# Reordered steps at the hand-over from the first token group to the second: weight sums, streamed forms, token statistics

## The chip, the cores and the metric

The kernel runs on one core of a Trainium2 chip. The metric is the device time of one execution in microseconds (us). TensorE is called PE in the profile, VectorE DVE, ScalarE ACT, GpSimd POOL and SyncE SP. SP issues nearly all of the DMAs in this kernel. Each engine works through one queue in order, so an instruction that waits holds up all that stand behind it on its engine.

## The reference

Windowed attention with four sink tokens feeds a Fourier mix, a layer norm and a feed-forward net:

```python
# q, k, v: (4, 8, 768, 64) fp32; window 128, 4 sinks
a = softmax(mask(q @ k.T / 8));  x = (a @ v)            # as (4, 768, 512)
u = x + real(fft(fft(x, axis=1), axis=2))
un = (u - mean(u)) / sqrt(var(u) + 1e-6)                # per token
out = u + relu(un @ w_ch1) @ w_ch2                      # w_ch1 (512, 2048), w_ch2 (2048, 512)
```

There are 3072 tokens, which the feed-forward net takes as 6 groups of 4 blocks of 128 tokens. The products are worked out in fp32 precision: each operand is split into a high half and a low half (what the high half lacks), and each product takes three matmuls (high by high, high by low, low by high).

## The kernel before

**The stages.** Attention and the Fourier mix come first, and their tail overlaps the first blocks of the feed-forward net. The first token group (group 0) runs a loop `for f in range(NF)` over 16 blocks of 128 hidden units. A step of the loop multiplies block f (`ch1`, L703: 12 matmuls of 128x512, tile `h`, reading the group's transposed tokens `un_slots` and the weights' two halves `w_ring`), splits the result (`split`: L1192 on ACT writes the relu's high half into `h_sb`, L1193 on DVE the low half) and multiplies block f-1 by the second weight matrix (`ch2`, L1199: 12 matmuls, tile `o`).

**Weights in the same loop.** The raw weights come from HBM by SP (L621, three buffers `raw`) two steps ahead. `convert` works on each: three DVE instructions (L639, L640, L641), the high half on ACT (L650 for the first matrix into `w_ring`, L665 for the second into `w`), the low half on POOL (L651, L666). A later group doesn't use the first matrix itself but seven sums of its quarters ("forms", a Strassen-like scheme with 7 products in place of 8). So `combine_w1(p)` takes the pair p of blocks f = 2p and 2p+1: four POOL instructions on 256 columns (L677 to L680) write the sums `tq` from `tw`, and a step later `halves` splits them into `to` (ACT L685, POOL L686). L687 stores these to HBM (`wd`), L654 stores `w_ring` there.

**The second group's tokens.** `prepare_1` is a generator of 20 steps that readies group 1 while group 0 runs: four of statistics (DVE L530, L531), one of the deviation (`deviations`, L537 to L552, with one square root on ACT, L540, and the load of its table ahead of it), then for each block a normalisation on ACT (`un_make`, L562, L563) and a transposition (PE L571, tile `unt`; ACT copies it out at L1257 into `xf`), and seven of sums of the token quarters (`do_x`: DVE L1301 the sums, ACT L1295 the high halves, DVE L1298 the low halves `x`). From f = PREP on, each step of the loop takes three of them.

**Group 1.** From `with tc.manual_schedule()` on, the order of the program is that of the engines; before it, a scheduler sets the order on each engine, held only by edges such as `tc.issue_after`. Four passes (`it`) of seven products each (`product`, L1421: 12 matmuls of 128x256 into the banks pA, pB and pC) read one form each, which two DMAs of 256 KB stream from HBM into one of eight places (L1394; `w_c` in the former raw buffers, `w_t`, `w_q` and `w_h` in the former `to`, `tq` and `h_sb`). The DVE combines the products (L1535 to L1559), `halves` splits them into `hring`, which takes the memory of `un_slots`, and `unit` (L1449, 12 matmuls, tile `o`) multiplies by the second matrix. After the products come numbered steps, ten in a pass: `todo` has the statistics, the deviation, the normalisation (`make`, L565 on DVE) and the transposition (`turn`) of group 2; `w2_at` has sums of the second matrix (DVE L1469, POOL L1474 to L1477, ACT L1481, POOL L1482) for the groups after that. Groups 2 to 5 work with streamed forms too (L1421, L1598).

## Time and profile before

| what | us |
|---|---|
| median of 3 runs (lowest, highest) | 746.86 (746.4, 748.05) |
| the profiled execution, its own time | 747.63 |
| its span in the trace | 745.9 |
| PE busy | 715.6 (96%) |
| DVE busy | 560.5 (75%) |
| ACT busy | 357.3 (48%) |
| POOL busy | 274.4 (37%) |

1.73 us of the profiled execution lie outside the span. Times in the trace count from the span's start. "PEld" is the loading of weights into PE, which runs beside the matmuls; "SPq" is SP issuing a DMA. The granted PE clock, as a mean over the span, was 0.994 of full speed. A bracket at the end of a row of the timeline says how long the engine had been idle before the row and what it then waited for. PE is the engine with the most work by far, so the question for any change is where PE is idle, and for what.

### The profile page before, as it was taken

The numbers are of one execution on the slowest core, as the hardware profiler recorded it, in microseconds if no ns is written. First come the engines' busy times: TensorE is split into PE (matmuls) and PEld (weight loads), VectorE is DVE, ScalarE is ACT, GpSimd is POOL, SyncE is SP. The second block draws the span as 40 slices with busy tenths as digits, with TensorE's granted clock in tenths as the row PEclk, the third lists the DMA queues.
The fourth block names the chain that finished last, engine by engine and source line by source line (L and its number), as shares of the span: only waits on it lengthen the run. The fifth ranks groups of instructions, "written<-read, shape, count | busy, mean of one in ns | idle before, by whom it ended". The sixth has DMA issues, their size and how long they took to land.

```text
span 745.9 us, 15695 instructions
## 1 busy us (share of the span) xinstructions
PE 715.6 (96%) x5539; PEld 642.6 (86%) x5539; DVE 560.5 (75%) x1299; ACT 357.3 (48%) x901; POOL 274.4 (37%) x391
## 2 busy tenths in 40 slices
PE   8999998989979999898999999999999999999996
PEld 6776876867868888687989999999999999999996
DVE  7778578888899988858668667947697578846773
ACT  5887666766634537313324134534444245523541
POOL 3567467577557989824994000000000000000000
PEclk9999999999999999999999999999999999999998
DMA  9863525533207999779999798979974897759721
GB/s 304 289 173 106 149 73 165 174 94 103 86 21 237 328 346 330 277 277 385 374 301 327 246 348 277 313 239 379 375 242 167 321 378 261 255 205 390 269 98 62
DMA packets 109576, 181.69 MB, mean 244 GB/s; under 512 B 9868, under 2 KB 44812, under 8 KB 108336
## 3 DMA queue, kind: packets, MB, share of 16 engines
q1 hardware_dynamic: 109200, 176.83, 69.6%
q0 software_dynamic: 288, 3.76, 1.3%
q8 instruction: 46, 0.75, 0.4%
q14 instruction: 42, 0.34, 0.1%
HBM read 148.04 MB, written 32.51 MB: 242 GB/s over the span
## 4 chain that ended last, share of the span: by engine, by line
PE 50%; DVE 4%; ACT 1%; issue 1%; SPq 0%; DMA 0%; POOL 0%; DVEq 0%
PE pB L1421 10%; PE qB L1598 9%; PE pA L1421 7%; PE pC L1421 6%; PE qC L1598 6%; PE qA L1598 6%; PE o L1449 5%; DVE bn L530 1%; PE unt L571 1%; DVE hring L1193 0%; DVE x L1657 0%; DVE x L1660 0%; SPq L1394 0%; DVE un L565 0%; DVE stat L531 0%
## 5 line engine op out<-in xcount | busy, mean ns | idle before, releaser
L1620 ACT CAST hring<-x 128x512 fp32r<-128x512 f32 x92 | 57.0, 619 | 52.0 <-PE qB L1598 19.6
L811 ACT ACTIVATE sm<-sm,mx 128x132 f32<-128x132 f32 x192 | 75.9, 400 | 4.6 <-DVE mx L805 4.6
L1624 DVE TENSOR_TENSOR hring<-x,hring 128x512 fp32r<-128x512 f32 x92 | 63.4, 689 | 14.8 <-ACT hring L1620 9.3
L786 PE MATMUL s<-ring,q 64*128 64x260 f32 x320 | 49.0, 411 | 5.9 <-DVE mx L805 2.7
L805 DVE CUSTOM_DVE_ANT_0 sm<-s,mask 128x132 f32<-128x132 f32 x192 | 48.5, 293 | 6.2 <-DVE s L792 0.9
L703 PE MATMUL h<-un_slots,w_ring 128*128 128x512 f32 x192 | 49.7, 405 | 3.4 <-POOL w_ring L651 2.9
L703 PEld LDWEIGHTS h<-un_slots,w_ring 128*128 128x128 f32 x192 | 36.3, 194 | 12.4 <-POOL w_ring L651 4.1
L786 PEld LDWEIGHTS s<-ring,q 64*128 64x128 f32 x320 | 26.9, 185 | 18.2 <-issue 5.0
L1598 PE MATMUL qA<-w,hring 128*128 128x256 f32 x312 | 39.8, 279 | 0.0
L1449 PE MATMUL o<-w,hring 128*128 128x512 f32 x156 | 38.5, 393 | 1.3 <-ACT hring L1192 1.1
L850 ACT COPY pta<-pt 128x512 f32<-128x512 f32 x48 | 28.1, 585 | 24.1 <-PE pt L843 24.0
L881 PE MATMUL xt<-ptl,ldv 128*64 128x128 f32 x384 | 39.3, 285 | 0.0
L1199 PE MATMUL o<-w,h_sb 128*128 128x512 f32 x156 | 38.1, 392 | 0.0
L1598 PEld LDWEIGHTS qA<-w,hring 128*128 128x128 f32 x312 | 37.9, 189 | 0.0
L811 ACT ACTIVATION_READ_ACCUMULATOR sm<-sm,mx 128x1 f32 x192 | 36.7, 191 | 0.0
L792 DVE COPY_PREDICATED s<-older,s 128x256 f32<-128x256 uint8 x80 | 33.7, 421 | 3.1 <-PE s L786 3.1
L859 POOL TENSOR_SCALAR_AFFINE_SELECT ptl<-pta 128x512 f32<-128x512 f32 x48 | 31.5, 655 | 11.6 <-ACT pta L850 11.6
L1598 PE MATMUL qB<-w_c,hring 128*128 128x256 f32 x288 | 35.2, 281 | 0.0
L1449 PEld LDWEIGHTS o<-w,hring 128*128 128x128 f32 x156 | 28.5, 188 | 7.5 <-ACT hring L1192 1.3
L881 PEld LDWEIGHTS xt<-ptl,ldv 128*64 128x64 f32 x384 | 22.1, 136 | 14.6 <-issue 4.8
L1598 PEld LDWEIGHTS qB<-w_c,hring 128*128 128x128 f32 x288 | 34.5, 189 | 0.0
L1199 PEld LDWEIGHTS o<-w,h_sb 128*128 128x128 f32 x156 | 29.1, 188 | 6.1
(296 smaller groups left out, 1965.3 us busy)
## 6 DMA issues: line engine op xcount, KB each, us to landing
w_c<-wd SPq DMA_DIRECT2D x96, 256.0 KB, 5.0
w_h<-wd SPq DMA_DIRECT2D x76, 256.0 KB, 5.1
w_t<-wd SPq DMA_DIRECT2D x70, 256.0 KB, 4.7
raw<-in_moe_w_ch_dram SPq DMA_DIRECT2D x32, 512.0 KB, 4.5
w_c<-td SPq DMA_DIRECT2D x48, 256.0 KB, 4.6
w_q<-wd SPq DMA_DIRECT2D x38, 256.0 KB, 5.0
wd<-to SPq DMA_DIRECT2D x8, 1024.0 KB, 6.4
ldv<-in_v_dram SPq DMA_DIRECT2D x28, 256.0 KB, 3.3
```

The costliest lines, as they stand in the source:

```text
L703: T.matmul(ps[:, :tb], a[cc], x[:, :, cc, :], start=n == 0, stop=n == 3 * NCC - 1)
L786: T.matmul(ps[:, j, :P + W], st["q", g][rows, hp, :], keys(g, 2 * hp + j), start=True, stop=True)
L792: V.copy_predicated(ps[:, :, P + NS:P + W], older[qi > 2], ps[:, :, 0:P])
L805: V.tensor_tensor_reduce(sm[:, h % 4], ps[:, j, P:P + W], mask[min(qi, 3)], -SCALE, 3.0e38, ALU.add, ALU.min, accum_out=mx[:, 0, h:h + 1])
L811: A.activation(sm[:, h % 4], sm[:, h % 4], AF.Exp, bias=mx[:, 0, h:h + 1], scale=-1.0, accum_out=mx[:, 1, h:h + 1])
L881: T.matmul(ps[D * j:D * j + D, p, :], st["v", kb(g) - i][:, h, :], a[:, h % 4, :], start=i == 0, stop=i == n - 1)
L1199: T.matmul(po[i], a[:, P * i:P * i + P], x, start=f == 0 and n == 0, stop=f == NF - 1 and n == 2)
L1421: T.matmul(ps[:, 256 * j:256 * j + 256], w[:, j, a, cs], x[:, xs], start=BANK.index(BANK[k]) == k and j == c == m == 0, stop=j == c == 1 a ...
L1449: T.matmul(po[i], h[:, a, j, ts_], x, start=first and j == m == 0, stop=last and j == 1 and m == 2)
L1598: T.matmul(ps[:, 256 * t:256 * t + 256], h[:, a, j, P * t:P * t + P], x, start=BANK.index(BANK[k]) == k and c == t == j == m == 0, stop=c ...
L1620: A.copy(hi, x)
L1624: V.tensor_tensor(*args, op=ALU.subtract)
```

## The change

It has four parts.

1. The steps of `prepare_1` are spread by a table: none in the step of f = 12, and the seven sums of the token quarters at f = 13 to 15 rather than up to f = 12. Each step is issued no earlier than the latest relu on ACT and the latest low half on DVE.
2. `combine_w1` issues its sums behind the low half of block 2p+1 on POOL, and two sums of 256 columns become one of 512. There are three instructions (L679, L680, L681 in the new kernel) for four.
3. The first four streamed forms (NH = 4) are loaded into `hring`, the memory of `un_slots`, as soon as `ch1` of the last block has read it, and not into `w_c` and `w_t`. The next three go to `w_c`. The last stores (`w_ring` and `to` of the last pair) stand on SP behind these seven forms. The order of the places after that is `w_q`, `w_t`, `w_t`, `w_h`.
4. Group 2's statistics, square root, normalisation and transposition move from the steps 0 to 14 to the steps 3 to 24, so that its first transposition stands in the second pass.

How this moves POOL at the blocks f = 12 and 13 (`tw_4007` before, `tw_3992` after; `tq` and `to` are the sums and the halves of the pair): before,

```order
L651 TENSOR_TENSOR w_ring<-tw_4007,w_ring 128x2x256
L677 TENSOR_TENSOR tq_4090<-tw_4007 128x256
L679 TENSOR_TENSOR tq_4090<-tw_4007 128x256
L678 TENSOR_TENSOR tq_4090<-tw_4007,tq_4090 128x256
L651 TENSOR_TENSOR w_ring<-tw_4007,w_ring 128x2x256
L680 TENSOR_TENSOR tq_4090<-tw_4007,tq_4090 128x256
L666 TENSOR_TENSOR w_1_4075<-cv_4067,w_0_4074 128x512
L666 TENSOR_TENSOR w_1_4087<-cv_4078,w_0_4086 128x512
L686 TENSOR_TENSOR to_4091<-tq_4090,to_4091 128x2x256 x2
L651 TENSOR_TENSOR w_ring<-tw_4131,w_ring 128x2x256
```

and after, with the two halves of the pair before (`to_3951`) parted:

```order
L687 TENSOR_TENSOR to_3951<-tq_3950,to_3951 128x2x256
L651 TENSOR_TENSOR w_ring<-tw_3992,w_ring 128x2x256
L687 TENSOR_TENSOR to_3951<-tq_3950,to_3951 128x2x256
L651 TENSOR_TENSOR w_ring<-tw_3992,w_ring 128x2x256
L679 TENSOR_TENSOR tq_4074<-tw_3992 128x512
L680 TENSOR_TENSOR tq_4074<-tw_3992,tq_4074 128x256
L681 TENSOR_TENSOR tq_4074<-tw_3992,tq_4074 128x256
L666 TENSOR_TENSOR w_1_4059<-cv_4051,w_0_4058 128x512
L666 TENSOR_TENSOR w_1_4071<-cv_4062,w_0_4070 128x512
L687 TENSOR_TENSOR to_4075<-tq_4074,to_4075 128x2x256
L651 TENSOR_TENSOR w_ring<-tw_4113,w_ring 128x2x256
L687 TENSOR_TENSOR to_4075<-tq_4074,to_4075 128x2x256
```

Both low halves of the first matrix now stand ahead of the pair's sums; before, three of the four sums stood between them. The low half of the next block (`tw_4113`) stands behind one half of the sums' split now, and behind both before.

On SP at the end of the first group (`wd_69` and on are the stored weights in HBM), before:

```order
L687 DMA wd_75<-to_4091 128x2048
L654 DMA wd_76<-w_ring 128x1536
L1394 DMA w_c_4268<-wd_69 128x512
L1394 DMA w_c_4268<-wd_70 128x512
L687 DMA wd_76<-to_4200 128x2048
L1394 DMA w_c_4269<-wd_69 128x512
L1394 DMA w_c_4269<-wd_70 128x512
```

and after, from the last of the eight loads into `hring` on (they stand right behind the store of `to_4075`):

```order
L1356 DMA hring<-wd_70 128x512
L1356 DMA w_c_4266<-wd_69 128x512
L1356 DMA w_c_4266<-wd_70 128x512
L1356 DMA w_c_4267<-wd_69 128x512
L1356 DMA w_c_4267<-wd_70 128x512
L1356 DMA w_c_4268<-wd_69 128x512
L1356 DMA w_c_4268<-wd_70 128x512
L654 DMA wd_76<-w_ring 128x1536
L688 DMA wd_76<-to_4179 128x2048
L1356 DMA w_q<-wd_71 128x512
```

The second form's loads no longer stand behind the store of the last pair's sums.

On PE at block 9 of the first group, where group 1's first transposition (`unt_0`) stands, before:

```order
L1199 MATMUL o_0_3243<-w_1_3706,h_sb_3788 128x512
L1199 MATMUL o_0_3244<-w_1_3706,h_sb_3788 128x512
L571 MATMUL unt_0_3895<-ident,un_4_3842 128x128 x4
L703 MATMUL h_9_3910<-un_slots,w_ring 128x512 x12
L1199 MATMUL o_0_3241<-w_0_3810,h_sb_3858 128x512
```

and after:

```order
L1200 MATMUL o_0_3243<-w_1_3703,h_sb_3784 128x512
L1200 MATMUL o_0_3244<-w_1_3703,h_sb_3784 128x512
L704 MATMUL h_9_3899<-un_slots,w_ring 128x512 x3
L571 MATMUL unt_0_3890<-ident,un_4_3837 128x128 x4
L704 MATMUL h_9_3899<-un_slots,w_ring 128x512 x9
L1200 MATMUL o_0_3241<-w_0_3806,h_sb_3853 128x512
```

It has moved three matmuls back on PE. What it reads has moved further on the other engines: group 1's square root (ACT L540, with its table load) stood behind the relu of block 3 in the before kernel, and stands between the relus of blocks 7 and 8 now. Group 2's square root stood on ACT ahead of the relu that feeds the first `unit`; now it stands behind the four relus of the first pass. Group 2's `unt_0` stood on PE behind the first `unit`; now it stands behind the third.

The diff, cut to its core:

```diff
-PREP_N = 3
+PREP_N = {6: 3, 7: 3, 8: 2, 9: 2, 10: 2, 11: 1, 13: 2, 14: 2, 15: 3}
...
-                    G.tensor_tensor(d[1], tf, f32(d[0]), op=ALU.subtract)
+                    state["lo", f] = G.tensor_tensor(d[1], tf, f32(d[0]), op=ALU.subtract).ins
...
-                G.tensor_tensor(q[:, 1], b12, b11, op=ALU.subtract)
+                with tc.issue_after(state["lo", 2 * p + 1]) if p else ExitStack():
+                    G.tensor_tensor(q[:, 1:3], t[:, 1].rearrange("p (h c) -> p h c", h=2), t[:, :, :256], op=ALU.subtract)
                 G.tensor_tensor(q[:, 0], b22, q[:, 1], op=ALU.subtract)
-                G.tensor_tensor(q[:, 2], b22, b12, op=ALU.subtract)
                 G.tensor_tensor(q[:, 3], b21, q[:, 0], op=ALU.subtract)
...
+            NH = 4
+            def place(n):
+                return hring[:, n] if n < NH else places[(n - NH) % NWS]
...
                 ps = hp.pop(0) if f < 2 else ch1(0, f, unT0)
+                if f == NF - 1:
+                    hring = npool.tile([P, 4, 2, 2, 256], F32R, tag="un_slots", name="hring", bufs=1)
+                    for n in range(NH):
+                        load(n)
...
-                for _ in range(PREP_N if f >= PREP else 0):
-                    next(steps, None)
+                for _ in range(PREP_N.get(f, 0)):
+                    with tc.issue_after(state["h_lo"]), tc.issue_after(state["relu"]):
+                        next(steps, None)
...
+            with tc.issue_after(state["load"]):
+                for n in range(NH, NH + LDB):
+                    load(n)
             for i in sorted(stores):
-                for fn in stores.pop(i):
-                    fn()
+                with tc.issue_after(state["load"]) if i > 2 * NF else ExitStack():
+                    for fn in stores.pop(i):
+                        fn()
...
-                    load(n + NWS)
+                    if n >= NH:
+                        load(n + NWS)
...
-                todo = {0: [(statistics, 0)], 1: [(statistics, 1, 2)], 2: [(statistics, 3)], 3: [(deviate, 7)], 5: [(deviate,), (make, 0)],
-                        7: [(turn, 0, *banks[1][:2]), (make, 1)], 9: [(turn, 1, *banks[1][:2]), (make, 2)],
-                        12: [(turn, 2, *banks[0][:2]), (make, 3)], 14: [(turn, 3, *banks[0][:2])]}
+                todo = {3: [(statistics, 0)], 4: [(statistics, 1)], 6: [(statistics, 2)], 7: [(statistics, 3)], 8: [(deviate, 1)],
+                        9: [(deviate, 1)], 10: [(deviate,)], 11: [(make, 0)],
+                        12: [(turn, 0, *banks[0][:2]), (make, 1)], 14: [(turn, 1, *banks[0][:2]), (make, 2)],
+                        22: [(turn, 2, *banks[1][:2]), (make, 3)], 24: [(turn, 3, *banks[1][:2])]}
```

## The prediction

> **What bounds the kernel now.** I read the page's chain by engine first, then the windows of busy time, then what PE waited for between 215 and 350 us, and last the timelines of PE, POOL, DVE, ACT and SP there.

> ```profile
> PE 50%; DVE 4%; ACT 1%; issue 1%; SPq 0%; DMA 0%; POOL 0%; DVEq 0%
> ...
> 350.00:400.00 50.00, 50.00 (x320) 45.02 (x319) 37.00 (x37) 16.91 (x29) 48.71 (x44) 1.00 1.02 339
> ...
> PE h L703 <- POOL w_ring L651: 2.9, 2, 1.5
> PE pB L1421 <- DMA w_c<-wd: 1.3, 1, 1.3
> PE o L1449 <- ACT hring L1192: 1.1, 1, 1.1
> ...
> PE pB L1421 <- ACT xf L1257: 1.0, 1, 1.0
> ```

> The chain is PE. The second line is a window (length, then busy us of PE, weight loads, DVE, ACT and POOL, then clock, DMA share, GB/s): behind 350 PE has nothing to gain. The wait lines (total, times, longest) name four causes at the hand-over, which are the places that the change touches. There PE's idle time counts in full, since behind it PE runs without gaps. PE itself shows what each costs, as extra time from one start to the next:

> ```profile
> 277.06 2.92 PE L1199 MATMUL o<-w,h_sb 128*128 128x512 f32 x12
> 279.82 0.60 PE L571 MATMUL unt<-ident,un 128*128 128x128 f32 x4
> ...
> 292.56 2.99 PE L703 MATMUL h<-un_slots,w_ring 128*128 128x512 f32 x12
> ...
> 305.95 2.56 PE L703 MATMUL h<-un_slots,w_ring 128*128 128x512 f32 x10 [1.36 <-POOL w_ring L651]
> ...
> 313.23 2.56 PE L703 MATMUL h<-un_slots,w_ring 128*128 128x512 f32 x10 [1.49 <-POOL w_ring L651]
> ...
> 318.39 2.93 PE L703 MATMUL h<-un_slots,w_ring 128*128 128x512 f32 x12
> ...
> 326.67 1.58 PE L1421 MATMUL pA<-x,w_c 128*128 128x256 f32 x12
> 329.55 1.69 PE L1421 MATMUL pB<-x,w_c 128*128 128x256 f32 x12 [1.30 <-DMA w_c<-wd]
> ...
> 332.50 1.59 PE L1421 MATMUL pA<-x,w_t 128*128 128x256 f32 x12
> 333.93 1.57 PE L1421 MATMUL pB<-x,w_t 128*128 128x256 f32 x12
> ...
> 339.90 0.60 PE L571 MATMUL unt<-ident,un 128*128 128x128 f32 x4
> ...
> 346.27 1.61 PE L1421 MATMUL pA<-x,w_h 128*128 128x256 f32 x12
> 348.85 1.68 PE L1421 MATMUL pB<-x,w_c 128*128 128x256 f32 x12 [0.96 <-ACT xf L1257]
> ```

> Twelve matmuls of 128x512 take 2.76 us from start to start (277.06 to 279.82), twelve of 128x256 1.43 (332.50 to 333.93).

> **The change, part by part.** *Sums behind the low halves.* From 292.56 to 318.39 PE does eight sets of 2.76, 22.08 us, in 25.83: 3.75 lost, in the main before `h`'s third matmul, twice. The cause stands on POOL and DVE:

> ```profile
> 301.20 1.06 POOL L677 TENSOR_TENSOR tq<-tw 128x256 f32<-128x256 f32 x1 [2.48 <-DVE tw L641]
> ...
> 304.62 1.28 POOL L651 TENSOR_TENSOR w_ring<-tw,w_ring 128x512 fp32r<-128x512 f32 x1
> ...
> 309.37 2.57 POOL L686 TENSOR_TENSOR to<-tq,to 128x512 fp32r<-128x512 f32 x2
> ...
> 313.12 0.75 POOL L677 TENSOR_TENSOR tq<-tw 128x256 f32<-128x256 f32 x1
> ...
> 294.04 1.82 DVE L1301 TENSOR_TENSOR xf<-xf 128x512 f32<-128x512 f32 x1
> ...
> 300.39 0.67 DVE L641 SCALAR_TENSOR_TENSOR tw<-raw,cw 128x512 int32<-128x512 int32 x1
> ```

> Block 13's converted weight is there at 301.06 (300.39 + 0.67). Three sums, 301.20 to 304.62, then stand ahead of its low half, which ends at 305.90; PE goes on at 305.95. Even with the DVE as late as this, the low half behind an ACT cast (0.6) would now end at 301.06 + 0.6 + 1.28 = 302.9, while PE wants it at 305.95 - 1.36 = 304.6. That wait goes. For block 14, POOL then has the wide sum (1.28, as for 512 columns in L651), two sums at 0.75, two low halves of the second matrix at 1.3, one half of `to` at 1.28 and the low half itself, 1.28: 7.9 us, so 310.8, against PE's need, the 1.36 earlier, at 313.23 - 1.49 - 1.36 = 310.4. With the DVE as late as before, 0.4 of the 3.75 would stay. But the x sums that stand ahead of this conversion leave it: three of L1301's form lie between 294.04 and 300.39, at up to the first one's 1.82, so the conversion is some 3 to 5 us earlier, and the wait is gone. I take 3.75; bounds 3.3 to 3.75. The merged sum saves some 0.2 us of POOL, which is off PE's path.

> *The first forms into `hring`.* 326.67 to 329.55 is 2.88, so 1.45 over a product. The chain of waits shows what released it:

> ```profile
> 322.60 1.27 POOL to L686
> ...
> 324.72 0.93 SPq L1394
> ...
> DMA to landing us min/median/max: 5.2/5.2/5.2
> ...
> DMA to landing us min/median/max: 3.4/3.4/3.4
> ```

> The second form's load stood on SP behind the store of POOL's last split, which ended at 323.87. From issue to landing it took 5.2 us (the first landing line; the second is the first form's, 7 us earlier). Now SP waits only for the last `ch1`, which ends two sets, 5.52 us, before the first product. With 3.4 to landing the first form is there 2 us early or so. The seven forms then have to keep up: at the 339 GB/s of the window, 512 KB take 1.55 against a product of 1.43, so 0.8 us is lost over seven forms, within the lead. At the spacing of the row of 324.72 (0.93 a DMA) the tenth would be issued 8.4 us after the first and land at 11.8, while the fifth form is wanted at 5.52 + 5.72 = 11.2: 0.6 us late. I take 1.45, bounds 0 to 1.45. The late stores of `wd_76` are read in pass 3 only, 40 us later; that lag is their cover.

> *Group 2's steps later.* 333.93 + 1.43 = 335.36, and the unit's 2.76 would end at 338.12, but `unt` starts at 339.90: 1.78 lost. Group 2's square root on ACT waited for its statistics, with the relu behind it; now it stands behind the relus. And from 346.27 to 348.85 1.15 over a product was lost, since the second pass's pB took the bank of `unt_1` while ACT's copy was outstanding; that transposition now lies in pass 2 and in the other bank. Bounds 1.4 to 1.78 and 0.6 to 1.15 (the DVE still has the statistics there); I take the full values.

> Gains: 3.75 + 1.45 + 1.78 + 1.15 = 8.1 us.

> *Cost one: group 1's `unt_0` within block 9.* Before, PE got to it at 279.82 and its normalisation was long done. Now:

> ```profile
> 243.88 1.28 ACT L540 ACT_TABLE_LOAD   x1
> 245.17 0.21 ACT L540 ACTIVATE stat<-stat 128x4 f32<-128x4 f32 x1
> ...
> 254.98 0.73 ACT L563 ACTIVATE un<-un,stat 128x512 f32<-128x512 f32 x1 [0.46 <-DVE stat L552]
> ...
> 276.53 0.69 DVE L639 TENSOR_SCALAR cw<-raw 128x512 int32<-128x512 int32 x1 [0.72 <-DMA raw<-in_moe_w_ch_dram]
> ...
> 269.11 0.43 SPq L621 DMA_DIRECT2D raw<-in_moe_w_ch_dram  x1
> DMA to landing us min/median/max: 4.2/5.5/7.2
> ```

> The deviation now follows block 8's first conversion on the DVE, which I put at 276.4: the DVE did this conversion just before the row at 276.53, and one more statistic of group 1 stands beside it. Table load 1.28, root 0.21: 277.9. Then block 8's relu on ACT (0.6) and four tiny DVE steps among block 8's conversions, which take 2 us each: the factor is there at 281.0, and one pass of `un` (0.73) ends at 281.8. PE is at `unt_0` three matmuls after 279.82, at 280.5. Wait 1.3; bounds 0 (the DVE idled 0.72 here, so it may come earlier) and 3.0 (where that load lands after 7.2 us and not the 5.5 of the median).

> [...]

> *Cost two: group 2's `unt_0` behind the third unit.* PE is there 9 products and 3 units after the first product's start T0: 12.87 + 8.28 = 21.15. Its normalisation waits on this:

> ```profile
> 347.69 0.63 ACT L1192 ACTIVATE hring<-tmp 128x512 fp32r<-128x512 f32 x1 [3.12 <-DVE tmp L1559]
> ...
> 348.69 1.14 ACT L1481 CAST tmp<-tmp 128x512 fp32r<-128x512 f32 x2
> 349.74 0.59 ACT L1533 COPY tmp<-pA 128x512 f32<-128x512 f32 x1
> ...
> 350.63 0.69 DVE L1535 TENSOR_TENSOR tmp<-pB,tmp 128x512 f32<-128x512 f32 x1 [1.13 <-PE pB L1421]
> ```

> The pass's last relu started 21.0 after T0 = 326.67, of which PE's stalls are 3.2: T0 + 17.8. The root (0.21) and two casts (1.14) and the copy (0.59) follow the relu's 0.63 on ACT, then the DVE's 0.69 and a normalisation, 0.54 where nothing disturbs it: T0 + 21.6. Statistics that now lie later in the pass may add 1, normalisations that leave it take off up to 1.5. I take a wait of 0.8, bounds 0 and 3.

> Net: 8.1 - 1.3 - 0.8 = 6.0. The profiled execution's 747.63 becomes 741.6 (span 745.9 to 739.9, 1.73 around it unchanged); it stands 0.77 above the median, so the median should come to 746.86 - 6.0 = 740.9.

> **The rivals.** (a) Both transpositions are ready in time: gain 8.1, 738.8. For it: the DVE's free time; against it: each chain above ends behind PE by its rows.
> (b) The streamed forms still come late by the 1.45 lost now: 742.3. For it: the DMA engines are busy all through (a share of 1.02 in that window) and the spacing of 0.93; against it: the lead of 5.5 us.
> (c) The x sums, now at f = 13 to 15, meet POOL's last sums, and the low halves of x are late for the first product: 1.82 for 0.68 three times is 3.4 us more DVE there; about half uncovered gives 1.7, so 742.6. For it, L1301 at 1.82 beside a POOL at work, and L677 at 1.06 then and 0.75 alone.
> [...]
> (d) POOL's sums of the second matrix set the pace of group 1. POOL is busy 48.71 of the window's 50 us and PE doesn't wait, but PE comes some 4 us earlier against them. If ACT's casts behind POOL then hold its relus, up to 2.5 of that is given back: 743.4.
> (e) ACT stands still behind the table load for as long again (1.28): 742.2. Against it: the root's start at 245.17, right behind the load's end. [...]
> (f) The parts cancel within what a measurement of this kernel can tell, 0.2% (1.5 us): the two new waits at their upper bounds, 3.0 and 3, and (b) as well would leave 0.7.
> (g) Slower, by one mechanism: `unt_0` in block 9. Its chain hangs on a raw load issued at 269.11, with 4.2 to 7.2 us to landing (5.5 as a median), then DVE, table load, DVE, ACT. PE can't pass it, so each us costs one. The gain is gone when `un` comes 6.0 us after 281.8, at 287.8, and it is slower by over 0.2% from 289.3. The spread of landings gives 1.7 only (7.2 for 5.5); it would need the DVE and ACT steps to lie behind a further block's conversions.

> **How the numbers follow.** My forecast 0.41 (own range 739.5 to 742.4), (a) 0.16, (b) 0.11, (c) 0.06, (d) 0.09, (e) 0.02, (f) 0.07, (g) 0.08. Faster by over 0.2%: the first six, 0.85; within: (f), 0.07; slower: (g), 0.08. The range goes from 738.2, (a) with a little more from an emptier DVE in the attention's tail (two L530 leave it), to 745.0, 1.6 above (d) for the costs' upper bounds; (f) and (g) lie outside.

> **What the profile would show.** Right: no PE wait on L651's successor after 300 us; the loads into `hring` issued right after the last `ch1`, no wait on a DMA in the first seven products; the first unit without a wait on a relu; waits before `unt` of 1.3 near 281 and 0.8 at T0 + 21. Wrong: a gap of over 3 us at one of these transpositions, waits of the products on forms or on x, or waits of group 1's units on ACT behind POOL's sums.

## The result, and the profile after

The changed kernel is slower. Its median is 758.34 us (755.94 to 759.84, 6 runs) against 747.1 (746.4 to 751.21, 6 runs) for the kernel before on the same chip: a ratio of 1.0145, interval 1.0123 to 1.0167, some 11 us where 6 us less were forecast. The profiled execution took 759.84 with a span of 758.1, so the two traces differ by 12.2 us of span. All times below "in the trace" are of such single profiled executions.

The page of the changed kernel, its busy times first and then its chain by engine:

```profile
PE 720.9 (95%) x5539; PEld 647.7 (85%) x5539; DVE 563.8 (74%) x1299; ACT 356.6 (47%) x901; POOL 269.4 (36%) x383
...
PE 69%; DVE 14%; DMA 5%; POOL 3%; issue 3%; ACT 3%; SPq 1%; DVEq 0%; ACTq 0%; POOLq 0%
```

PE is busy 5.3 us longer (715.6 before) with the same 5539 matmuls, at a mean granted clock of 0.986 and not 0.994, and the rest of the 12.2 is idle time. What PE waited for between 215 and 360 us (total, times, longest):

```profile
PE pA L1435 <- ACT tmp L1549: 5.3, 1, 5.3
PE unt L571 <- ACT un L563: 2.9, 1, 2.9
PE h L704 <- DVE h_sb L1194: 1.9, 3, 1.0
```

The two low-half waits, the late form, the relu and the copy that stood in this view before are gone, all five. In their place stand two longer waits, the first of which no line of the prediction names, and a third just behind 360 us (2.62). The last line, the DVE's low halves of `h_sb`, stood there with one wait of 0.6 before. PE's timeline of the changed kernel shows them with what follows each:

```profile
282.41 0.86 PE L704 MATMUL h<-un_slots,w_ring 128*128 128x512 f32 x3
286.13 1.12 PE L571 MATMUL unt<-ident,un 128*128 128x128 f32 x4 [2.86 <-ACT un L563]
286.90 3.53 PE L704 MATMUL h<-un_slots,w_ring 128*128 128x512 f32 x9
290.27 2.93 PE L1200 MATMUL o<-w,h_sb 128*128 128x512 f32 x12
...
330.51 1.52 PE L1435 MATMUL pA<-x,hring 128*128 128x256 f32 x12
...
340.07 2.93 PE L1435 MATMUL pA<-x,hring 128*128 128x256 f32 x12 [5.32 <-ACT tmp L1549]
...
361.55 1.08 PE L571 MATMUL unt<-ident,un 128*128 128x128 f32 x4 [2.62 <-DVE un L565]
362.29 2.70 PE L1435 MATMUL pC<-x,w_t 128*128 128x256 f32 x12
```

Behind each wait the next matmuls take twice their usual time: a product 2.93 and 2.70 and not 1.52, four transpositions 1.08 and 1.12 and not 0.60. The windows of busy time right behind the waits (length, then PE, weight loads, DVE, ACT, POOL, then the granted clock, DMA share, GB/s) show why:

```profile
286.13:290.20 4.07, 4.07 (x13) 3.43 (x14) 2.55 (x4) 2.70 (x5) 3.54 (x3) 0.58 1.01 389
...
340.07:342.80 2.73, 2.73 (x12) 2.73 (x13) 2.01 (x4) 0.62 (x1) 0.00 (x0) 0.50 0.97 386
...
361.55:364.80 3.25, 3.25 (x16) 3.25 (x17) 2.58 (x3) 1.62 (x3) 2.40 (x3) 0.53 1.08 373
```

The granted clock was 0.58, 0.50 and 0.53 there. So each of these waits cost its idle time and about 1.5 to 1.9 us more, from work at half speed.

What released the longest wait, by the chain that ended last (start, length, what):

```profile
327.67 5.18 DMA hring<-wd
...
332.91 6.42 DMA wd<-w_ring
...
339.44 0.59 ACT tmp L1549
...
340.07 2.94 PE pA L1435 x12
```

and by ACT's timeline at the same place:

```profile
327.49 1.13 ACT L1296 CAST x<-xf 128x512 fp32r<-128x512 f32 x2
339.44 0.58 ACT L1549 COPY tmp<-pA 128x512 f32<-128x512 f32 x1 [10.81 <-DMA wd<-w_ring]
```

ACT's next instruction is the copy of the first product out of bank pA, and it stands still for 10.81 us. That product had ended at 332.03 (330.51 + 1.52), so the last 7.4 us are the wait for a store. The code says why: `w_ring` and `tmp` are tiles of one memory.

```python
state["ring"] = npool.tile([P, 2, 4, 2, 256], F32R, tag="ring", name="w_ring", bufs=1)
...
tmp = npool.tile([P, 8, 512], F32, tag="ring", name="tmp", bufs=1)   # p1c = tmp[:, 0]
```

The copy is the first write to `tmp`; the last store of `w_ring` is the last read of `w_ring`. The change put this store on SP behind 14 loads of forms. It was issued at 332.91 and had landed only at 339.33. Three products went on in the three banks, then PE needed bank pA again and idled.

### The profile page after: what moved, and what is told of

Read it like the earlier page. It is cut to its first block, busy times and chain, and to the rows that moved or that the text cites. A ratio compares the mean times of both kernels' runs of the same rounds, so it can differ in the third digit from the quotient of the medians.

```text
span 758.1 us, 15676 instructions
## 1 busy us (share of the span) xinstructions
PE 720.9 (95%) x5539; PEld 647.7 (85%) x5539; DVE 563.8 (74%) x1299; ACT 356.6 (47%) x901; POOL 269.4 (36%) x383
## 4 chain that ended last, share of the span: by engine, by line
PE 69%; DVE 14%; DMA 5%; POOL 3%; issue 3%; ACT 3%; SPq 1%; DVEq 0%; ACTq 0%; POOLq 0%
PE pB L1435 9%; PE qB L1614 9%; PE pA L1435 7%; PE pC L1435 6%; PE qA L1614 6%; PE qC L1614 6%; PE o L1464 5%; PE xt L882 4%; PE s L787 4%; PE h L704 3%; PE o L1200 2%; PE pt L844 2%; DMA raw<-in_moe_w_ch_dram 1%; PE unt L571 1%; PE za L398 1%
## 5 line engine op out<-in xcount | busy, mean ns | idle before, releaser
L1435 PE MATMUL pB<-x,w_c 128*128 128x256 f32 x348 | 45.2, 283 | 0.0
L1435 PEld LDWEIGHTS pB<-x,w_c 128*128 128x128 f32 x348 | 43.2, 191 | 0.0
```

Source lines behind the costliest of these rows:

```text
L1435: T.matmul(ps[:, 256 * j:256 * j + 256], w[:, j, a, cs], x[:, xs], start=BANK.index(BANK[k]) == k and j == c == m == 0, stop=j == c == 1 a ...
```

## The experiments

Each ratio is against the kernel before on the same chip; rows with the same time before shared a chip and its runs.

| kernel | median us (runs) | before | ratio, interval |
|---|---|---|---|
| e1_ring_store | 750.35 (9) | 747.23 | 1.0053, 1.003 to 1.0076 |
| e2_prep_old | 760.27 (6) | 747.23 | 1.0159, 1.013 to 1.0188 |
| e3_todo_old | 755.91 (6) | 747.23 | 1.0109, 1.007 to 1.0148 |
| x123_sums_forms | 756.84 (6) | 747.23 | 1.0121, 1.0092 to 1.015 |
| f1_unt1_later | 750.55 (12) | 746.6 | 1.005, 1.0029 to 1.007 |
| f2_unt2_later | 750.88 (12) | 746.6 | 1.0041, 1.0016 to 1.0066 |
| f3_both_later | 748.54 (12) | 746.6 | 1.0019, 0.9998 to 1.0041 |
| f4_both_sums_old | 748.09 (12) | 746.6 | 1.0017, 0.9995 to 1.0039 |
| g1_w2_earlier | 751.56 (6) | 746.22 | 1.007, 1.0048 to 1.0092 |
| g2_before_steps | 745.97 (12) | 746.22 | 0.9996, 0.9981 to 1.0011 |
| h1_before_store_late | 747.2 (12) | 746.22 | 1.0006, 0.9993 to 1.0019 |
| f3_again | 748.9 (1) | 747.16 | one run |
| k1_w2_two_earlier | 750.74 (12) | 747.16 | 1.0049, 1.0034 to 1.0065 |
| k2_steps_forms | 747.02 (12) | 747.16 | 0.9996, 0.9978 to 1.0013 |
| m1_casts_later | 745.19 (12) | 746.29 | 0.9974, 0.9957 to 0.9992 |
| m2_casts_earlier | 745.61 (12) | 746.29 | 0.9992, 0.998 to 1.0003 |

### The store of `w_ring` ahead of the forms

The changed kernel with only this store put back ahead of the loads:

```diff
                     hring = npool.tile([P, 4, 2, 2, 256], F32R, tag="un_slots", name="hring", bufs=1)
+                    for fn in stores.pop(2 * NF + 2, ()):
+                        fn()
                     for n in range(NH):
                         load(n)
```

> The changed kernel with one edit: the last store of w_ring is issued ahead of the streamed forms again, and not behind seven of them. Theory 1 (that store holds the memory that the pass's first copy of pA writes, so ACT's copy and PE behind it wait until it has landed): PE's wait of 5.32 us before the fourth product goes, and with it the slow clock behind it (1.3 + 0.6 us), so about 7 us less: 751.3. Rival (ACT's copy would be late anyway, behind casts of x that wait for the DVE's sums): at most 2 us less, 756.5. Rival (the store's traffic delays the forms): a wait on a form takes the place, 755.

Measured: 750.35, that is 8.0 us less than the changed kernel's median, which comes from another set of runs, or 6.9 us by the two ratios (0.92% of 747). In the timelines of this kernel, SP's store, ACT's copy and the fourth product and the third unit:

```profile
314.50 0.33 SPq L654 DMA_DIRECT2D wd<-w_ring  x1
...
328.83 0.59 ACT L1551 COPY tmp<-pA 128x512 f32<-128x512 f32 x1 [3.49 <-issue]
...
331.30 1.52 PE L1437 MATMUL pA<-x,hring 128*128 128x256 f32 x12
...
345.69 2.92 PE L1466 MATMUL o<-w,hring 128*128 128x512 f32 x12
```

The store is issued 18 us earlier, the copy waits for no store, and PE goes on. The first product starts at 327.22 here, so from it to the third unit PE needs 18.47 us; before it was 23.70 (326.67 to 350.37), after 25.50 (330.51 to 356.01). So the store's place cost 7.0 us in this stretch, which agrees with the 6.9 of the ratios. Another 3.3 between the two traces lie ahead of the first product, where the store can't act.

The same mechanism was tried the other way round, in the kernel before, with its `w_ring` store behind the first three loads of forms:

```diff
+            ring_store = stores.pop(2 * NF + 2)
...
+                if n == 2:
+                    with tc.issue_after(state["load"]):
+                        for fn in ring_store:
+                            fn()
```

> The kernel before with one edit: the last w_ring store issued behind the first three forms' loads. Theory 1 (ACT's copy of pA waits for that store, about 6 us after its issue): PE waits for the fourth product until about 335.5 in place of 332.5; the wait of 1.8 us at the first unit is partly covered by it: 1.5 to 4 us more than before, 748 to 751. Rival (the store costs nothing there, what the change lost at this place is due to hring): no change, 746.5 to 747.

Measured: no change (1.0006). ACT's copy and the fourth product of this kernel:

```profile
330.41 0.59 ACT L1538 COPY tmp<-pA 128x512 f32<-128x512 f32 x1 [9.14 <-PE pC L1426]
...
331.05 1.21 PE L1426 MATMUL pA<-x,w_t 128*128 128x256 f32 x8 [0.71 <-ACT tmp L1538]
```

The copy starts 2.9 us after the product that it reads has ended (327.50), where in the kernel before it followed at once. PE's wait is only 0.71 long, since here the store was issued at 323.98, 8.9 us earlier than after. The view puts the copy's release down to the end of `pC`, which the copy doesn't read; the store's landing, 6.4 us after its issue if it takes as long as in the changed kernel, falls at the same moment (330.4). So the trace agrees with the mechanism but doesn't name the store. The second form's wait (1.30 before) is gone, because the loads got ahead of the last `to` store. From the first product to the third unit this trace takes 24.52 us (325.92 to 350.44), 0.8 more than before and not the 1.5 to 4 that were expected, and the median can't tell it. The two places of the store together suggest that the price depends on how far behind it is put.

### The tables of steps, each put back

Both are the changed kernel with one part as before.

```diff
-PREP_N = {6: 3, 7: 3, 8: 2, 9: 2, 10: 2, 11: 1, 13: 2, 14: 2, 15: 3}
+PREP_N = {f: 3 for f in range(6, 16)}
...
-                    with tc.issue_after(state["h_lo"]), tc.issue_after(state["relu"]):
-                        next(steps, None)
+                    next(steps, None)
```

> The changed kernel with the old table of group 1's steps (three at each f from 6 on, no edges behind the relu and the low half). Theory 1: the transposition in block 9 no longer waits (2.86 us and about 1.8 us of slow clock behind it), 4.6 us less; if the later raw loads at the end of the attention (2.6 us in the profile of the change) come from the steps' place too, up to 7 us less. With the x sums back at f up to 12, 0 to 0.4 us of the low half's wait returns. So 751 to 754. Rival (the wait came from the raw load on SP, not from the place of the steps): no more than 1 us less, 757.5.

Measured: 760.27, a miss: it was to be faster. `unt`'s wait for ACT falls from 2.9 to 0.8 (the store's wait, 5.5, and that of group 2's `unt_0`, 2.8, stay), but block 14's weights are late again, by PE's timeline of this kernel:

```profile
311.42 0.77 PE L704 MATMUL h<-un_slots,w_ring 128*128 128x512 f32 x2 [0.78 <-ACT w_ring L650]
314.33 3.58 PE L704 MATMUL h<-un_slots,w_ring 128*128 128x512 f32 x10 [2.15 <-POOL w_ring L651]
```

This set takes 7.07 us, from 310.64 to the next set's start at 317.71, and not 2.76: the lost 4.3 is more than the 3.75 of both waits before, and this with POOL's new order in place. The second table:

```diff
-                todo = {3: [(statistics, 0)], 4: [(statistics, 1)], ...
+                todo = {0: [(statistics, 0)], 1: [(statistics, 1, 2)], ...   # as before
```

> The changed kernel with the old table of group 2's steps in the first pass. Theory 1: the wait at group 2's first transposition in the second pass (2.62 us and 1.5 us of slow clock) goes; the relu behind the square root and the copy in pB's bank (1.78 and 1.15 us in the kernel before) come back in part: 1 to 4 us less, 754.3 to 757.3. Rival (what the DVE has to do sets the pace, wherever group 2's steps stand): no change, 758.

Measured: 755.91, 2.4 us under the changed kernel, which the two intervals don't tell apart. Group 2's late `unt_0` is gone; of the two old waits the copy's is back (0.9) and the relu's is not, and the store's wait stays (5.5).

With the store ahead and both tables old, that is with POOL's sums and the forms in `hring` alone:

> The sums behind the low halves and the forms in hring alone: the w_ring store ahead of the forms, and both tables of steps old. Theory 1 (these two parts are worth what the forecast gave them, 3.4 and 1.45 us, and everything lost came from the store and the two tables): 4 to 5 us less than the kernel before, 742.5. Rival (the new order on POOL costs the end of the attention 2.6 us through SP's and the DVE's queues): 745.

Measured: 756.84, a miss by 14 us. PE's timeline of this kernel at block 14:

```profile
314.60 1.07 PE L704 MATMUL h<-un_slots,w_ring 128*128 128x512 f32 x2 [1.87 <-ACT w_ring L650]
317.48 4.47 PE L704 MATMUL h<-un_slots,w_ring 128*128 128x512 f32 x10 [1.80 <-POOL w_ring L651]
```

The set takes 9.06 us (312.73 to 321.79) at a clock of about 0.52. So putting the sums behind the low halves does not remove this wait while the DVE still works on the x sums; and the 1.87 are not POOL's at all: ACT's high half (313.93) follows the DVE's conversion, which ends at 313.90. The first product starts at 332.85 in this trace, 6.2 later than before; the other 3.3 us of its span's excess lie behind it, where the relus of group 1's units are waited for three times, 4.0 in all.

### The two transpositions later

From here on the store stands ahead, as in the first experiment. Group 1's turns one block later, group 2's first two turns two steps later, and both:

```diff
-PREP_N = {6: 3, 7: 3, 8: 2, 9: 2, 10: 2, 11: 1, 13: 2, 14: 2, 15: 3}
+PREP_N = {6: 3, 7: 3, 9: 2, 10: 2, 11: 2, 12: 1, 13: 2, 14: 2, 15: 3}
```

```diff
-                        12: [(turn, 0, ...), (make, 1)], 14: [(turn, 1, ...), (make, 2)],
+                        14: [(turn, 0, ...), (make, 1)], 16: [(turn, 1, ...), (make, 2)],
```

> The change with the w_ring store ahead of the forms (750.35 in the run before), and group 1's transpositions one block later (none of its steps at f = 8, the rest of them up to f = 12). Theory 1 (the transposition in block 9 is reached before its normalisation is done, and PE waits 2.45 us there): the wait goes, 2.6 us less, 747.8. Rival (the raw loads come late, and another wait on them takes its place): 749.5 to 750.5.

> The change with the w_ring store ahead of the forms (750.35), and group 2's first two transpositions two steps later in the second pass (14 and 16 for 12 and 14). Theory 1 (PE reaches unt_0 2.96 us ahead of its normalisation, and the idle time turns the clock down for what follows, another 1.5): both go, 4.4 us less, 746.0. Rival without the clock: 3.0 less, 747.4. Rival (the DVE is late as a whole, and the next unit or copy waits in its place): 749 to 750.

> Both edits of the two runs beside this one. Theory 1: the waits are independent, 7.0 us less than 750.35, so 743.4, some 4 us faster than the kernel before: what the change's four parts are worth without the three waits. Rival (POOL's sums of the second matrix give part of it back when PE comes earlier): 745 to 746.

Measured: 750.55, 750.88 and 748.54, three misses by the first theory of each. Each removes its own wait from the trace, but one alone brings nothing that these runs can tell; both together bring it to within 0.2% of the kernel before, and not below it. With both, PE reached the first product at 322.67, 4.0 us earlier than before, in the profiled execution (744.86, the fastest of the twelve). It reached group 3's first transposition at 422.55:

```profile
322.67 1.52 PE L1437 MATMUL pA<-x,hring 128*128 128x256 f32 x12
...
422.55 0.60 PE L571 MATMUL unt<-ident,un 128*128 128x128 f32 x4
```

That is 99.88 us, against 99.50 before (326.67 to 426.17), although no form, no copy and no root is waited for any more. What PE waits for in this stretch, and the timelines of POOL, ACT and PE there:

```profile
PE o L1466 <- ACT hring L1193: 2.8, 2, 1.7
...
355.07 0.74 POOL L1491 TENSOR_TENSOR tmp<-sums_r 128x256 f32<-128x256 f32 x1 [3.44 <-DMA td<-tmp]
...
356.66 0.62 ACT L1498 CAST tmp<-tmp 128x512 fp32r<-128x512 f32 x1 [5.95 <-POOL tmp L1492]
...
358.05 0.62 ACT L1498 CAST tmp<-tmp 128x512 fp32r<-128x512 f32 x1 [0.77 <-POOL tmp L1494]
...
359.25 0.50 PE L1466 MATMUL o<-w_gh,hring 128*128 128x512 f32 x1 [1.66 <-ACT hring L1193]
```

POOL's sums of the second matrix wait for their memory till its store has landed (`td`), ACT's casts wait for POOL, and a unit's relu stands behind these casts on ACT. This is rival (d) of the prediction. Without the three old waits (1.45, 1.78 and 1.15) the stretch should have been 4.4 shorter; the two new ones take 2.8, and some 2 us more go in shorter delays that no run separates. A second profile of the same kernel, taken because its fastest run had been the profiled one:

> The run with both transpositions later once more, for a second profile: its first one, 744.86, was the fastest of twelve runs with a median of 748.5. Theory (late raw loads at the end of the attention): a run near the median shows PE waits for low halves of h at blocks 5 to 7 and reaches block 9 at 281 or later, not at 279.3. Rival (the time is lost in group 1): block 9 at 279.3, and larger waits behind 325 us.

Measured: 748.9, 4.0 us more. Its trace has the relu waits too (1.9 in all) and other ones: 1.8 for block 15's relu (`h_sb`), 1.9 for the DVE's low halves of `h_sb` in three earlier blocks, 0.6 for POOL. Block 9 starts at 280.69 and not at 279.28, as the first theory has it, and the first product at 327.16, 0.5 later than in the kernel before; from it to group 3's transposition it takes 99.00 us. So in this execution there is no gain at the hand-over either. In this kernel the same waits come and go from run to run.

Are POOL's new order and the merged sum worth anything, once the x sums have left the DVE? The kernel with both turns later, and its four sums in the order of before:

> As the run with both edits, and combine_w1's sums in their old form: four sums of 256 columns, not held behind the low half. Theory 1 (with the x sums gone from the DVE, the conversions come early enough that three sums ahead of block 13's low half cost little): 0 to 1 us more than the run with both edits. Rival (the place of the sums on POOL is what removed the waits on the low half): 2 to 3 us more.

Measured: 748.09 against 748.54: nothing that can be told.

### The second matrix's sums earlier

If ACT's casts stand ahead of the relus, their steps could start earlier, by 4 steps and by 2:

```diff
-  for t, fn in ((5 + 3 * p if p else 6, whole_w2), (7 + 3 * p, sums_w2), (9 + 3 * p, split_w2), ...
+  for t, fn in ((1 + 3 * p if p else 2, whole_w2), (3 + 3 * p, sums_w2), (5 + 3 * p, split_w2), ...
```

> The change with the w_ring store ahead of the forms and both transpositions later, and now with all steps of the second matrix' sums (w2_at) four steps earlier in group 1. Theory 1 (POOL, idle for some 16 us at the start of group 1 and then without a pause, paces group 1 once PE comes earlier; ACT's casts behind POOL hold the relus, and PE waits 1.66 and 1.16 us and restarts slowly): those waits go, about 4 us less than the run with both transpositions later (748.5), so 744.5, faster than the kernel before by 2 us. Rival (the stores of these sums wait for the DMA engines, and starting earlier moves the wait only): 748 to 749.

> The change with the w_ring store ahead of the forms and both transpositions later (748.5), with the second matrix' sums two steps earlier, not four (four made the DVE late in the first pass: PE waited 4.05 us there). Theory 1 (POOL's sums hold ACT's relus and pace group 1): the waits of 1.66 and 1.16 us become smaller, the DVE's lateness of the first pass doesn't come, 2 to 4 us less than 748.5: 744.5 to 746.5. Rival (every place that these sums can take costs the same elsewhere): 748 to 749.5.

Measured: 751.56 and 750.74, both slower than with the steps where they were. With 4 steps the relu waits behind POOL go, but PE waits 4.0 us ahead of them for a bank that the DVE has not emptied, so whether they went for the earlier sums or for the later PE is not separated; with 2 steps both kinds are there. PE's waits from 320 to 430 us, first of the former and then of the latter kernel:

```profile
PE pC L1437 <- DVE tmp L1569: 4.0, 1, 4.0
```

```profile
PE pC L1437 <- DVE tmp L1569: 2.9, 2, 1.9
...
PE o L1466 <- ACT hring L1193: 1.7, 1, 1.7
```

### Parts that are worth keeping, in the kernel before

Only group 1's steps late, then also the first three forms' loads ahead of the last `to` store (in `w_c`, as before), POOL and group 2 as they were:

```diff
-PREP_N = 3
+PREP_N = {6: 3, 7: 3, 9: 2, 10: 2, 11: 2, 12: 1, 13: 2, 14: 2, 15: 3}
...
+                    with tc.issue_after(state["h_lo"]), tc.issue_after(state["relu"]):
+                        next(steps, None)
```

> The kernel before with the new places of group 1's steps alone (with the transpositions one block later than in the change): x sums at f = 13 to 15, all else old. Theory 1 (it is the x sums on the DVE that made the low halves late, not the sums on POOL): the two waits of 1.36 and 1.49 us on the low half go, 2.5 to 3.5 us less than before, 743.5 to 744.5. Rival (the sums on POOL made them late): both waits stay, 746.5. Rival (the second form then waits longer for its load behind the last pair's store, since POOL isn't done earlier): 1 to 2 us less, 745.3.

> The kernel before with two of the gains alone: group 1's steps late, transpositions with a block to spare (745.97 alone), and the first three forms' loads ahead of the last store of the sums, into w_c as before. The w_ring store stays ahead of them; group 2's steps, POOL's sums and hring stay as they were. Theory 1 (the wait of 1.3 us on the second form goes, and POOL's pace isn't reached since PE comes at most 4 us earlier with 1.8 and 1.15 lost behind): 744 to 744.7, faster than the kernel before by 1.5 to 2.2 us. Rival (what is gained at the first product is lost behind it): 746.

Measured: 0.9996 and 0.9996, no change. In both the waits of 1.36 and 1.49 are gone with POOL's order untouched. A shorter one at L651 stands earlier instead, 0.82 at 286.62 and 0.48 at 287.14, and a new one appears at block 15, of 1.0 and 1.76. ACT's timeline of the second kernel, and the DVE's sum that the cast waits for:

```profile
321.94 0.62 ACT L1295 CAST x<-xf 128x512 fp32r<-128x512 f32 x1 [2.19 <-DVE xf L1301]
322.47 0.59 ACT L1192 ACTIVATE h_sb<-h 128x512 fp32r<-128x512 f32 x1
...
320.13 1.78 DVE L1301 TENSOR_TENSOR xf<-xf,sx 128x512 f32<-128x512 f32 x1
```

Block 15's relu stands behind a cast of x, which waits for a DVE sum that takes 1.78. So one step was moved over this relu, to either side:

```diff
-..., 13: 2, 14: 2, 15: 3}
+..., 13: 2, 14: 1, 15: 4}     # m1_casts_later
+..., 13: 3, 14: 3, 15: 1}     # m2_casts_earlier
```

> As the run of two gains alone (747.02 against 747.16), but the step with the third sum of x and its cast at f = 15 and not at f = 14, so that on ACT the relu of block 15 stands ahead of that cast. Theory 1 (that relu waits behind a cast whose sum the DVE hasn't done, PE waits 1.76 us for it, and this is what ate the gain at the end of group 0): 1.5 to 1.8 us less, 745.3, faster than the kernel before by 0.2 to 0.3%. Rival (x is then late for the first products, by as much): 747.

> As the run beside it, but the x sums earlier: three steps at f = 13, three at 14, one at 15. Theory 1 (the DVE has to do the same work ahead of the last conversions): the low halves of blocks 14 and 15 wait again, the relu of block 15 behind four casts; 746.5 to 748. Rival (the DVE has time at f = 13): 745.5.

Measured: 0.9974 (0.9957 to 0.9992) and 0.9992. With the cast later, block 15's `ch2` and the one before it run on into the first product without a wait:

```profile
317.30 5.67 PE L1199 MATMUL o<-w,h_sb 128*128 128x512 f32 x24
322.81 1.58 PE L1428 MATMUL pA<-x,w_c 128*128 128x256 f32 x12
```

This version beats both kernels, by 0.26% of the one before, with the interval's end close to nothing; against the version without this step (0.9996, on another chip) the intervals overlap, so the step's own share is not settled. Its profiled execution (742.57) is one of its fast ones, so the 3.9 us at the first product are not what its median keeps.

## Why the prediction was wrong, and where it was right

Where the 12.2 us came from, by the same instructions in both traces, and what the prediction's terms had put there. The marks are the starts of block 9 (with the transposition that stood ahead of it before), of the `ch2` behind it, of the first product, of the third unit, and of a later unit at 408.28 before and 419.32 after:

| stretch | before | after | difference | forecast |
|---|---|---|---|---|
| start to block 9 | 279.82 | 282.41 | +2.6 | 0 |
| to block 9's `ch2` | 3.22 | 7.86 | +4.6 | +1.3 |
| to the first product | 43.63 | 40.24 | -3.4 | -3.75 |
| to the third unit | 23.70 | 25.50 | +1.8 | -5.1 |
| to the later unit | 57.91 | 63.31 | +5.4 | +1.5 |
| to the end | | | +1.1 | 0 |

The forecast column counts 0.72 for the two transpositions that leave the fourth stretch and come into the fifth. It sums to -6.0, so 18.2 us lie between forecast and trace.

**The step that failed** is the sentence on the late stores, that they are read in pass 3 only and that this lag is their cover. It asked who reads what the store writes, not what the store itself reads and who writes there next. The fourth stretch is 6.9 worse than forecast; the wait of 5.32 and the 1.9 of slow clock behind it make 7.2, and the store put back gave some 7 us. None of the seven rivals had it either; the slower one was pinned to another place. With the store put back the kernel is still 0.5% slower than the one before, so the store is not the only step that failed; the others follow.

**Sums behind the low halves**: 3.4 of 3.75 came, so the size was right, but the cause was not POOL's order. The waits return with that order when the x sums stay at f up to 12 (4.3 and 6.3 lost in the two kernels), and go without it when the sums move later. The prediction's remark that the conversion would be earlier was the term that carried it.

**Forms, root and bank**: all three waits are gone, after as in the run with only the store ahead. There the stretch to the third unit is 5.2 shorter, against 1.45 + 1.78 + 1.15 + 0.72 = 5.1 forecast. But the 4.4 of the three waits are given back further on: with no wait on a transposition left, the stretch from the first product to group 3's transposition is as long as before, in both profiles. The forecast added up removed waits and took it that PE would then run on. Rival (d) was to take back 2.5 at most: POOL, the store of its sums and ACT's casts hold two relus for 2.8 (1.9 in the second profile), and the rest of the 4.4 is not separated.

**Group 1's `unt_0`**: mis-sized at 1.3. PE waited 2.86 (within the bound of 3.0) and then ran at 0.58 of the clock, which cost another 1.8. The chain itself was the one described; its start was late: block 8's first conversion, put at 276.4, ended at 280.26 (279.59 + 0.67). SP's and the DVE's timelines of the changed kernel:

```profile
263.07 9.39 SPq L465 DMA_DIRECT2D ud<-us  x5
272.52 0.42 SPq L621 DMA_DIRECT2D raw<-in_moe_w_ch_dram  x1
...
277.19 0.69 DVE L639 TENSOR_SCALAR cw<-raw 128x512 int32<-128x512 int32 x1 [1.67 <-DMA raw<-in_moe_w_ch_dram]
```

The load that the prediction placed at 269.11 was issued at 272.52, 3.4 later: the five stores ahead of it on SP began 0.9 later than before (262.15) and took 9.39 and not 6.92. Of the first stretch's 2.6, 0.8 were there by block 4 (249.80 and not 249.03); the late store in the kernel before, which changes nothing that early, stands as late there (249.79), so this is within what executions differ by. The other 1.8 came at blocks 5 to 7, where PE waited twice for the DVE's low halves (0.96 and 0.31). No run isolates why these and the stores took longer, so that part stays open.

**Group 2's `unt_0`**: mis-sized at 0.8. The wait was 2.62 (bound 3), and 1.5 more went to the clock of 0.53. The timelines of the DVE and POOL ahead of it:

```profile
357.21 1.22 DVE L548 SCALAR_TENSOR_TENSOR stat<-stat 128x4 f32<-128x4 f32 x1
358.46 1.19 DVE L550 TENSOR_TENSOR stat<-stat 128x4 f32<-128x4 f32 x1
...
357.11 2.52 POOL L1497 TENSOR_TENSOR tmp<-tmp 128x512 fp32r<-128x512 f32 x2 [3.84 <-ACT tmp L1496]
```

The two tiny steps take 1.2 each beside POOL's casts. In group 1's chain of the same kernel L548 took 0.16 at 283.15, where POOL idled from 282.42 to 283.96. The prediction had left these steps out of this sum.

**The clock** was in no term. Each wait was priced at its idle time; behind the three waits of the changed kernel 5.2 more were lost (1.8, 1.9 and 1.5).

**Rival (c)**, x sums that meet POOL's last ones, was right on the place, but not on the victim: it is block 15's relu behind a cast and not the first product, with 0.4 to 1.8 in eight traces of the versions with late steps. In the changed kernel itself PE didn't wait for it. The 0.75 of L677 that the prediction calls "alone" (313.12) stood beside the DVE's L640, 0.70 from 313.11 on.

What stays open: the last 1.1 us; and why the kernels with late steps spread more from run to run (748.54 is a median between 744.86 and 751.55). The second profile shows which waits come and go, not what moves them. Part of it may be the clock, by what the last section finds.

## What to carry to other kernels

Before a store is put off, look up whose memory it reads and which tile takes that memory next; its reader at the far end is only half of what depends on it. Price a wait of PE by its idle time and by a possible restart at half clock, which stood here behind a wait of 1.87 us and took 1.5 to 1.9 us more behind three waits of the changed kernel, and follow each removed wait to the next queue that works in order: here a relu behind a cast behind a sum behind a store took back 2.8 of the 4.4 us that were won in group 1. A forecast that adds up removed waits needs a second sum, the one of the engine that is nearly as late in the following stage.

## What was not expected of the hardware

The restart of the clock is not a matter of the wait's length alone. In the first experiment a wait of 2.45 and one of 2.96 stand in one trace, and the windows right behind them read:

```profile
284.35:286.90 2.55, 2.55 (x13) 2.19 (x14) 2.45 (x4) 2.52 (x5) 2.02 (x2) 1.00 0.98 396
351.56:354.86 3.30, 3.29 (x16) 3.30 (x17) 2.58 (x3) 1.62 (x3) 2.45 (x3) 0.53 1.03 391
```

Full clock behind the first and 0.53 behind the second. A longer wait, of 3.00 in the kernel with group 1's turns later, was followed by full clock:

```profile
351.47:354.00 2.53, 2.53 (x22) 2.53 (x23) 2.53 (x3) 1.63 (x3) 2.15 (x3) 1.00 1.01 370
```

while 1.87, in the kernel with the store ahead and both tables old, was followed by 0.53:

```profile
314.60:317.48 2.88, 1.08 (x3) 0.36 (x3) 2.01 (x4) 0.62 (x1) 2.88 (x4) 0.53 0.96 391
```

| wait | stretch of 3.41 us | PE busy there | clock in the stretch behind each |
|---|---|---|---|
| 2.86 (changed kernel) | 282.69 to 286.10 | 0.59 | 0.50 |
| 5.32 (changed kernel) | 333.89 to 337.30 | 0.86 | 0.50 |
| 2.62 (changed kernel) | 357.79 to 361.20 | 1.14 | 0.50 |
| 2.45 (store ahead) | 279.57 to 282.98, 282.98 to 286.40 | 2.33, 2.05 | 1.00, 1.00 |
| 2.96 (store ahead) | 347.83 to 351.24 | 0.78 | 0.50 |
| 1.87 (both tables old) | 311.38 to 314.79 | 1.54 | 0.50 |

The traces of the kernel before and of the changed one, divided at this spacing from 10 to 735 us, show the same: the six stretches with 0.59 to 1.63 us of PE's work were each followed by one at 0.50, and all others, with 1.92 or more, by one at 1.00. For the wait of 3.00 no fall near it shows where these stretches lie, and no run moves a wait in time and leaves all else, so what decides was not isolated. What a wait costs differs from run to run: at group 2's `unt_0` one of 2.62 had 0.53 behind it, which took 1.5 us more, and one of 3.00 had 1.00.

The same two-input DVE instruction (L1302 in the changed kernel) takes 0.68 at 340.72, where POOL is idle, and 1.77 at 324.67 beside a working POOL; a step on 128x4 elements (L548, above) takes 0.16 or 1.22. The difference is about 1.1 in both. It is not always the DVE that takes longer: in the kernel before, L1298 took 0.67 at 302.19, and a sum of POOL that began 0.04 later (L679) took 1.24, where the same sum took 0.75 at 313.81. What one engine waits for beside the other, no trace names.
